# Retention and a snake feed-forward on one core: where transposes, stores, loads, one product, one relay and one output piece stand in the program of batches 1 to 4

## The chip, the core and the metric

The kernel runs on one core of a Trainium2 chip. The metric is the device time of one launch in microseconds (us). Before the change the median of three runs is 295.25 us (295.24, 295.25 and 296.3). A change of about 0.5% (1.5 us) is what a measurement of this kernel can tell from none.

The engines are named as in the profile: PE is the matrix engine (PEld its weight loads), DVE the vector engine, ACT the scalar engine, POOL the GpSimd engine, SP the engine that only issues DMAs. Each runs its own list of instructions in order; they meet at semaphores.

## The reference

```python
def _attn_ref(q, k, v):               # batch 8, heads 8, sequence 576, head size 64
    scores = scale * np.matmul(q, k.transpose(0, 1, 3, 2))
    rel = pos[:, None] - pos[None, :]
    Dmat = np.where(rel >= 0, gamma[:, None, None] ** rel[None, :, :], 0.0)
    return np.matmul(scores * Dmat, v)

def _moe_ref(x, w_in, w_out, alpha):  # x: 4608 tokens x 512; hidden size 2048
    h = x @ w_in
    s = np.sin(alpha * h)
    g = h + s * s / (alpha + 1e-09)
    return g @ w_out
```

The retention output of all heads, laid side by side, is the `x` of the feed-forward part. Inputs and output are float32.

## The kernel before, in words

The tokens are worked in nine **blocks** of 512: block n < 8 is the first 512 tokens of batch n, block 8 gathers the last 64 tokens of all batches. The feed-forward part of a block is cut into sixteen **units** of 128 hidden features, and for each unit there is:

- `project(n, fc, tag, part)`: PE multiplies `w_in` with the block's `xT` into the PSUM bank `tag` (L541), in one piece of 512 tokens or in two parts of 256;
- `sine(n, fc)`: ACT takes the sine out of that bank (L549);
- `square(n, fc, eng)`: ACT, DVE or POOL squares it in SBUF (L558, or L560 on DVE and POOL);
- `product(n, fc)`: DVE joins the square with the bank into `gT` (L565). Only then is the bank free for the next unit.

For blocks 0 and 1 the second matrix product is `gemm2(n, u, tag)` (L587): piece u of 16 does four of the sixteen hidden chunks of the 128-token column c = u // 4, and four pieces fill one bank. `finish(n, c)` copies that bank to an SBUF tile (L102 on ACT, L104 on DVE) and issues two stores on SP (L580). From block 2 on, seven products with sums and differences of weights take its place (`multiply`, L658); the weight differences come from `weigh` on POOL (L608).

Retention of batch b is done in two halves p of 256 tokens. `load(b, nm, p)` issues the 512 KB load of k, q or v on SP (L121); `cast(b, nm, p, eng, ys)` scales and narrows it to f16 on DVE or POOL (L181; plain for v: L102, L104), `ys` picking halves of the heads; from batch 2 on `crossed(b, p, nms)` issues a DMA transpose on SP (L205) that makes `kT` or `qT`. Then come `scores` (L363), `masked` (L375, DVE), `values` (L406), and the running state: `outer` (L298), `take_sum`, `next_sum`, `more` and `to_state` (L102, L327, L344, L345, L332), `add_states` (L428) and `keep`, which writes the block's `xT`.

`told(last, eng)` puts an empty instruction on an engine that waits for `last`, so that the engine goes no further until then (L250). With `relay=A_`, `values(p, False, ...)` puts such an instruction on ACT, and `values(p, True)`, which writes the same bank's other rows, waits for it on PE.

The order of everything is written out by hand between L746 and L1483 under a manual schedule: each call appends to the lists of the engines that it uses, in the order of the text. The change touches that list at L885 to L903 (units 10 to 15 of block 0), L969 to L1018 (end of batch 1, start of block 1, casts and transposes of batch 2, loads of batch 3) and L1118 to L1127 (transposes of batch 3, first load of batch 4). All SP work goes through one queue in that order.

Of the kernel before, what the change touches and what calls it, by code (L numbers as in the profile page):

```python
# [18 lines left out]
def kernel(  # L19
# [16 lines left out]
    nc = tc.nc  # L36
# [51 lines left out]
    V, A_, G_ = nc.vector, nc.scalar, nc.gpsimd  # L88
# [8 lines left out]
    def halves(n):  # L97
        return slice(64 * n, 64 * n + 64)
# [39 lines left out]
    def cast(b, nm, p, eng, ys=(0, 1)):  # L138
        t_ = raw[b, nm, p]
        if (b, nm, p) not in half:  # L140
            if p < 2:
                if nm == "k":
                    d_ = work.tile([P, 16 * D], F16, tag=f"k16{slot(b, p)}", bufs=1, name="k16")
                elif nm == "q":
                    n = order_of_q.index((b, p)) % 3 if b < 5 else 1 - p
                    d_ = work.tile([P, 16 * D], F16, tag=f"q16{n}", bufs=1, name="q16")
                else:
                    d_ = work.tile([P, 16 * D], F16, tag="v16", bufs=4, name="v16")
                d_ = (
                    d_.rearrange("p (h r d) -> p h r d", r=2, d=D)  # L150
                    if nm == "v"
                    else d_.rearrange("p (a r t d) -> p a r t d", a=4, r=2, t=2)
                )
            elif nm == "v":
                d_ = work.tile([P, H, D], F16, tag="vs16", bufs=B // 2, name="vs16")
            else:
                tag, n = ("qks16", 2) if b % 4 == 0 else (f"k16{int(nm == 'q')}", 1)
                d_ = work.tile([P, 4, 2, D], F16, tag=tag, bufs=n, name=nm + "s16")
            half[b, nm, p] = d_
        dst = half[b, nm, p]  # L160
        if p == 2:
            if nm == "v":
                copy(eng, dst.rearrange("p h d -> p (h d)"), t_.rearrange("p h d -> p (h d)"))
            else:
                eng.tensor_tensor(
                    dst.rearrange("p a t d -> p t a d"),
                    t_.rearrange("p (t a) d -> p t a d", t=2),
                    fac_s[nm].rearrange("p (t a) -> p t a", t=2).unsqueeze(3).to_broadcast([P, 2, 4, D]),
                    MULT,
                )  # L170
        elif nm == "v":
            h0, h1 = 4 * ys[0], 4 * ys[-1] + 4
            copy(
                eng,
                dst[:, h0:h1].rearrange("p h r d -> p (h r d)"),
                t_[:, h0:h1].rearrange("p h x -> p (h x)"),
            )
        else:
            a0, a1 = 2 * ys[0], 2 * ys[-1] + 2
            n = 2 * (a1 - a0)  # L180
            return eng.tensor_tensor(  # L181
                dst[:, a0:a1].rearrange("p a r t d -> p t (a r) d"),
                t_.rearrange("p (t a) x -> p t a x", t=2)[:, :, a0:a1].rearrange("p t a (r d) -> p t (a r) d", r=2),
                fac["halved k" if nm == "k" and b >= HALVED else nm]
                .rearrange("p (t x) -> p t x", t=2)[:, :, 2 * a0 : 2 * a1]
                .unsqueeze(3)
                .to_broadcast([P, 2, n, D]),
                MULT,
            )
# [58 lines left out]
    def told(last, eng):  # L248

        mark = eng.nop()  # L250
        order(mark, last)
        return mark
# [280 lines left out]
    def project(n, fc, tag, part=None):  # L533

        if n not in gT:
            gT[n] = work.tile([P, 2, FC, 256], F16, tag="gT", bufs=2, name="gT")
        if (n, fc) not in hps_of:
            hps_of[n, fc] = [bank(tag), None]
        cols = PART[part]
        for a in range(KT):  # L540
            matmul(  # L541
                hps_of[n, fc][0][:, cols], w_in16[:, a, fc * P : (fc + 1) * P], xs[n][:, a, cols],
                start=(a == 0 and part != 1), stop=(a == KT - 1), skip_group_check=True,
            )
# [9 lines left out]
    def square(n, fc, eng):  # L554
        s_t = hps_of[n, fc][1]
        ss_t = work.tile([P, 512], F16, tag="ss", bufs=4, name="ss_t")
        if eng is nc.scalar:
            nc.scalar.activation(ss_t, s_t, mybir.ActivationFunctionType.Square)  # L558
        else:
            eng.tensor_tensor(ss_t, s_t, s_t, MULT)  # L560
        hps_of[n, fc][1] = ss_t

    def product(n, fc):
        hps, ss_t = hps_of.pop((n, fc))
        nc.vector.scalar_tensor_tensor(  # L565
            gT[n][:, :, fc, :], ss_t.rearrange("p (t n) -> p t n", t=2), inva[:, fc : fc + 1],
            hps.rearrange("p (t n) -> p t n", t=2), MULT, ADD,
        )

    def rows_of(n, c):  # L570
        if n == 8:
            return out.rearrange("(b s) d -> b s d", s=S)[2 * c : 2 * c + 2, 512:576, :]
        r0 = 576 * n + 128 * c
        return out[r0 : r0 + 128, :].rearrange("(i r) d -> r i d", r=2)

    def finish(n, c, eng=None, cols=slice(0, 512), issue=(nc.sync, nc.sync)):
        osb = work.tile([P, 512], F32, tag="osb", bufs=4, name="osb")
        copy(eng or nc.scalar, osb[:, cols], ops[n, c, cols.start][:, cols])
        for r in range(2):
            issue[r].dma_start(rows_of(n, c)[r, :, cols], osb[halves(r), cols])  # L580

    def gemm2(n, u, tag, cols=slice(0, 512)):
        c, part = divmod(u, 4)
# [162 lines left out]
    with tc.manual_schedule():  # L746
# [139 lines left out]
        project(0, 10, "m0")  # L886
        sine(0, 10)
        square(0, 10, G_)
        told(cast(1, "k", 0, V, (1,)), G_)
        project(0, 11, "op")  # L890
        sine(0, 11)
        square(0, 11, A_)
        product(0, 10)
        product(0, 11)
        project(0, 12, "h2")
        sine(0, 12)
        square(0, 12, G_)
        project(0, 13, "h0")
        sine(0, 13)
        square(0, 13, A_)  # L900
# [69 lines left out]
        at[1].outer((1,), "m0")  # L970
        at[1].next_sum(2)
        at[1].to_state(2, V)
        at[1].take_sum(3, A_)
        at[1].values(1, False, "m1", relay=A_)
        gemm2(0, 7, "op")
        at[1].values(1, True)
        at[1].add_states(1)
        at[1].keep(1, A_)
        finish(0, 1)
        cast(2, "k", 1, V, (1,))  # L980
        cast(2, "k", 0, V)
        crossed(2, 0, "k")
        crossed(2, 1, "k")
        at[1].more(3)
        at[1].to_state(3, G_)
        cast(2, "v", 0, G_)
# [4 lines left out]
        weigh(2, 0, G_)  # L991
        project(1, 0, "m0", 0)
        project(1, 1, "h2", 0)
        project(1, 0, "m0", 1)
        sine(1, 0)
        project(1, 1, "h2", 1)
        square(1, 0, V)
        sine(1, 1)
        gemm2(0, 3, "h0")
        product(1, 0)  # L1000
        cast(2, "q", 0, V)
        crossed(2, 0, "q")
        load(3, "k", 1)
        finish(0, 0)
        square(1, 1, A_)
        project(1, 2, "m1", 0)
        project(1, 2, "m1", 1)
# [3 lines left out]
        project(1, 3, "h0")  # L1011
        sine(1, 3)
        crossed(2, 1, "q")
        load(3, "q", 1)
        load(3, "v", 0)
        load(3, "k", 0)
# [99 lines left out]
        sine(1, 15)  # L1116
        cast(3, "v", 1, A_, (0,))
        cast(3, "k", 0, V, (1,))  # L1118
        load(4, "k", 0)
        crossed(3, 0, "k")  # L1120
        cast(3, "v", 0, G_, (0,))
        cast(3, "v", 1, G_, (1,))
        at[2].more(3)
# [390 lines left out]
```

## Time and profile before

| | |
|---|---|
| median of the runs | 295.25 us (295.24 to 296.3) |
| the profiled execution | 296.25 us, of which the span of its instructions is 294.5 us |
| PE busy | 280.7 us, 95% of the span, granted clock 1.00 |
| DVE, ACT, POOL busy | 217.1, 211.3, 207.9 us |
| moved by DMA | 49.89 MB, mean 169 GB/s over the span |

In rows of the timeline the first two numbers are the start and the length in us, then engine, source line, operation, written tile <- read tiles, shape and how many instructions in a row were merged; what stands in square brackets is the idle time of the engine just before and what ended it. In the table of waits, the three numbers are the total in us, how many times, and the longest. Line numbers are those of the kernel before; in the changed kernel, lines from 582 on are six to eight higher.

### The profile page before, as it was taken

The numbers are of one execution on the slowest core, as the hardware profiler recorded it, in microseconds if no ns is written. First come the engines' busy times: TensorE is split into PE (matmuls) and PEld (weight loads), VectorE is DVE, ScalarE is ACT, GpSimd is POOL, SyncE is SP. The second block draws the span as 40 slices with busy tenths as digits, with TensorE's granted clock in tenths as the row PEclk, the third lists the DMA queues.
The fourth block names the chain that finished last, engine by engine and source line by source line (L and its number), as shares of the span: only waits on it lengthen the run. The fifth ranks groups of instructions, "written<-read, shape, count | busy, mean of one in ns | idle before, by whom it ended". The sixth has DMA issues, their size and how long they took to land.

```text
span 294.5 us, 8771 instructions
## 1 busy us (share of the span) xinstructions
PE 280.7 (95%) x3611; PEld 184.3 (63%) x3611; DVE 217.1 (74%) x299; ACT 211.3 (72%) x343; POOL 207.9 (71%) x198
## 2 busy tenths in 40 slices
PE   6799999989799999999999999999999999999993
PEld 5574455566544666676666666666666666665782
DVE  3859859999666689989686967686778495747861
ACT  3859733976849898787777778787868879887600
POOL 4888868999999989999997799679915800460000
PEclk9999999999999999999999999999999999999999
DMA  7999999999997887978798785778657101311225
GB/s 225 291 250 223 280 238 296 215 188 296 224 261 249 112 191 175 273 181 184 175 251 165 164 231 129 93 162 182 141 114 168 43 4 38 71 38 27 59 47 119
DMA packets 119159, 49.89 MB, mean 169 GB/s; under 512 B 69824, under 2 KB 118096, under 8 KB 119120
## 3 DMA queue, kind: packets, MB, share of 16 engines
q1 hardware_dynamic: 114528, 45.04, 65.2%
q0 software_dynamic: 4224, 4.19, 8.6%
q8 instruction: 28, 0.46, 0.7%
q10 hardware_dynamic: 368, 0.11, 0.2%
q14 instruction: 11, 0.09, 0.1%
HBM read 36.74 MB, written 9.44 MB: 157 GB/s over the span
## 4 chain that ended last, share of the span: by engine, by line
PE 75%; POOL 7%; DVE 6%; DMA 4%; ACT 3%; issue 2%; SPq 1%; ACTq 0%; POOLq 0%
PE hps L541 32%; PE hps L658 29%; PE ops L587 6%; DVE gT L565 2%; POOL T L608 2%; PE o L406 2%; PE sc L363 2%; DMA k<-in_k_dram 2%; DVE ret L375 2%; DMA qT<-q 2%; DVE k L181 2%; ACT s_t L549 1%; SPq L121 1%; POOL q L181 1%; PE kv L298 1%
## 5 line engine op out<-in xcount | busy, mean ns | idle before, releaser
L565 DVE SCALAR_TENSOR_TENSOR gT<-ss_t,inva,hps 128x512 f16<-128x512 f16 x144 | 105.2, 744 | 41.0 <-ACT ss_t L558 39.3
L549 ACT ACTIVATE s_t<-hps,alpha_t 128x512 f16<-128x512 f32 x144 | 96.5, 681 | 37.4 <-PE hps L541 37.0
L541 PE MATMUL hps<-xT,w_in 128*128 128x512 f16 (+1 forms) x604 | 121.3, 347 | 0.3
L541 PEld LDWEIGHTS <-w_in 128*128 128x128 f16 x668 | 63.7, 98 | 50.4 <-issue 1.2
L558 ACT ACTIVATE ss_t<-s_t 128x512 f16<-128x512 f16 x121 | 75.7, 630 | 3.4
L658 PEld LDWEIGHTS <-gT 128*128 128x128 f16 x656 | 63.9, 98 | 14.5
L630 POOL TENSOR_TENSOR gT<-gT,d 128x1024 f16<-128x1024 f16 x12 | 25.6, 2151 | 26.7 <-PE hps L658 26.0
L658 PE MATMUL hps<-T,gT 128*128 128x256 f16 x336 | 39.8, 273 | 0.0
L375 DVE TENSOR_TENSOR ret<-sc,mask 128x1024 f16<-128x1024 f32 (+1 forms) x32 | 35.0, 1119 | 6.4 <-PE sc L363 6.4
L658 PE MATMUL hps<-w_out,gT 128*128 128x256 f16 x320 | 38.2, 273 | 0.0
L678 DVE TENSOR_TENSOR osb<-osb,hps 128x512 f32<-128x512 f32 x35 | 24.0, 685 | 12.6 <-PE hps L658 11.3
L587 PE MATMUL ops<-w_out,gT 128*128 128x512 f16 x128 | 30.8, 380 | 0.7 <-DVE gT L565 0.7
L636 POOL TENSOR_TENSOR gT<-gT 128x1024 f16<-128x1024 f16 x12 | 25.3, 2128 | 0.0
L181 POOL TENSOR_TENSOR q<-q,cn 128x1024 f16<-128x1024 f32 (+1 forms) x16 | 25.2, 1590 | 0.1
L332 POOL TENSOR_TENSOR s<-kvs,cn 128x256 f16<-128x256 f32 x22 | 14.6, 664 | 8.2 <-ACT kvs L102 7.4
L587 PEld LDWEIGHTS <-gT 128*128 128x128 f16 x128 | 11.8, 98 | 13.1 <-issue 0.9
L345 POOL TENSOR_TENSOR kvs<-s,kvs 128x256 f32<-128x256 f32 x23 | 18.7, 812 | 1.8
L181 POOL TENSOR_TENSOR k<-k,cn 128x1024 f16<-128x1024 f32 (+1 forms) x11 | 18.8, 1709 | 0.0
L102 ACT COPY osb<-hps 128x512 f32<-128x512 f32 (+2 forms) x15 | 8.2, 549 | 13.5 <-PE hps L658 13.3
L102 ACT CAST xT<-o 128x1024 f16<-128x1024 f32 (+1 forms) x14 | 13.8, 989 | 4.0 <-PE o L428 4.0
L344 POOL TENSOR_TENSOR s<-kvs,cn 128x256 f32<-128x256 f32 x23 | 15.5, 673 | 1.6 <-DVE kvs L327 1.4
L541 PE MATMUL hps<-xS,w_in 128*128 128x512 f16 x64 | 15.0, 379 | 0.0
(78 smaller groups left out, 271.1 us busy)
## 6 DMA issues: line engine op xcount, KB each, us to landing
out_dram<-osb SPq DMA_DIRECT2D x70, 128.0 KB, 2.5
q<-in_q_dram SPq DMA_DIRECT2D x16, 512.0 KB, 6.0
k<-in_k_dram SPq DMA_DIRECT2D x10, 512.0 KB, 5.8
v<-in_v_dram SPq DMA_DIRECT2D x10, 512.0 KB, 6.6
k<-in_k_dram SPq DMA_DIRECT2D x24, 128.0 KB, 3.4
v<-in_v_dram SPq DMA_DIRECT2D x24, 128.0 KB, 3.6
w_in<-in_moe_w_in_dram POOLq DMA_DIRECT2D x4, 512.0 KB, 9.1
w_out<-in_moe_w_out_dram POOLq DMA_DIRECT2D x4, 512.0 KB, 9.5
```

The costliest lines, as they stand in the source:

```text
L102: eng.copy(d_, s_)
L181: return eng.tensor_tensor(dst[:, a0:a1].rearrange("p a r t d -> p t (a r) d"), t_.rearrange("p (t a) x -> p t a x", t=2)[:, :, a0:a1].rea ...
L375: made = nc.vector.tensor_tensor(ret.rearrange("p t (z x) -> p (t z) x", z=2)[:, :, 0:n], sc.rearrange("p t (z x) -> p (t z) x", z=2)[:, : ...
L541: matmul(hps_of[n, fc][0][:, cols], w_in16[:, a, fc * P : (fc + 1) * P], xs[n][:, a, cols], start=(a == 0 and part != 1), stop=(a == KT - ...
L549: nc.scalar.activation(s_t, hps, mybir.ActivationFunctionType.Sin, bias=0.0, scale=alpha_t[:, fc : fc + 1],)
L558: nc.scalar.activation(ss_t, s_t, mybir.ActivationFunctionType.Square)
L565: nc.vector.scalar_tensor_tensor(gT[n][:, :, fc, :], ss_t.rearrange("p (t n) -> p t n", t=2), inva[:, fc : fc + 1], hps.rearrange("p (t n) ...
L587: matmul(ops[n, c, cols.start][:, cols], gT[n][:, c // 2, fk, c % 2 * P : c % 2 * P + P], w_out16[:, fk, cols], start=(fk == 0), stop=(fk ...
L630: eng.tensor_tensor(self.part(0, 0, i), self.part(1, 1, i), self.d3[:, 4 * i : 4 * i + 4], SUB)
L636: eng.tensor_tensor(out_, self.part(1, 0, i), self.part(0, 0, i), SUB)
L658: matmul(self.ps[name][:, 256 * m + cols.start : 256 * m + cols.stop], left(j)[:, P * m : P * m + P], right(j)[:, cols], start=(tag is not ...
L678: nc.vector.tensor_tensor(out_, a, self.ps[ps], ADD)
```

## The change

Some pieces of work stand at other places of the list. What is computed and the number of instructions stay the same.

1. Block 0: `product(0, 11)` goes between the two DVE halves of the cast of k of batch 1, ahead of `product(0, 10)`. POOL's wait for the second half (`told`) goes behind POOL's square of unit 12.
2. Batch 1: the relay on ACT goes ahead of the copy of the fourth sum (`take_sum(3, A_)`).
3. Batch 2: the transpose of k, half 0, goes ahead of the stores of `finish(0, 1)`, and the transpose of k, half 1, behind the transpose of q, half 0, and the stores of `finish(0, 0)`.
4. Block 0's last piece of column 0, `gemm2(0, 3)`, goes ahead of the second parts of block 1's units 0 and 1; the copy of `finish(0, 0)` follows it on ACT, and only its stores (`store_0`) stay at the old place.
5. The load of k of batch 3, half 1, goes behind the last transpose of batch 2.
6. The transpose of k of batch 3, half 0, goes ahead of the first load of batch 4.

```diff
+    def finish(n, c, eng=None, cols=slice(0, 512), issue=(nc.sync, nc.sync), hold=False):
         osb = work.tile([P, 512], F32, tag="osb", bufs=4, name="osb")
         copy(eng or nc.scalar, osb[:, cols], ops[n, c, cols.start][:, cols])
-        for r in range(2):
-            issue[r].dma_start(rows_of(n, c)[r, :, cols], osb[halves(r), cols])
+        def store():
+            for r in range(2):
+                issue[r].dma_start(rows_of(n, c)[r, :, cols], osb[halves(r), cols])
+        if hold:
+            return store
+        store()
...
         square(0, 10, G_)
-        told(cast(1, "k", 0, V, (1,)), G_)
         project(0, 11, "op")
         sine(0, 11)
         square(0, 11, A_)
+        product(0, 11)
+        cast_k = cast(1, "k", 0, V, (1,))
         product(0, 10)
-        product(0, 11)
         project(0, 12, "h2")
         sine(0, 12)
         square(0, 12, G_)
+        told(cast_k, G_)
...
+        at[1].values(1, False, "m1", relay=A_)
         at[1].take_sum(3, A_)
-        at[1].values(1, False, "m1", relay=A_)
...
-        finish(0, 1)
         cast(2, "k", 1, V, (1,))
         cast(2, "k", 0, V)
         crossed(2, 0, "k")
-        crossed(2, 1, "k")
+        finish(0, 1)
...
         project(1, 0, "m0", 0)
         project(1, 1, "h2", 0)
+        gemm2(0, 3, "h0")
+        store_0 = finish(0, 0, hold=True)
         project(1, 0, "m0", 1)
         sine(1, 0)
         project(1, 1, "h2", 1)
         square(1, 0, V)
         sine(1, 1)
-        gemm2(0, 3, "h0")
         product(1, 0)
         cast(2, "q", 0, V)
         crossed(2, 0, "q")
-        load(3, "k", 1)
-        finish(0, 0)
+        store_0()
+        crossed(2, 1, "k")
...
         crossed(2, 1, "q")
+        load(3, "k", 1)
         load(3, "q", 1)
...
         cast(3, "k", 0, V, (1,))
+        crossed(3, 0, "k")
         load(4, "k", 0)
-        crossed(3, 0, "k")
```

On DVE, at the casts of k of batch 1 (tile `k_635`, from the loaded `k_361`), between the products of block 0 (`gT`):

```order
 L565 SCALAR_TENSOR_TENSOR gT<-ss_t,inva,hps 128x2x256 x9
-L181 TENSOR_TENSOR k_635<-k_361,cn 128x2x4x64 x2
-L565 SCALAR_TENSOR_TENSOR gT<-ss_t,inva,hps 128x2x256 x4
+L181 TENSOR_TENSOR k_635<-k_361,cn 128x2x4x64
+L565 SCALAR_TENSOR_TENSOR gT<-ss_t,inva,hps 128x2x256
+L181 TENSOR_TENSOR k_635<-k_361,cn 128x2x4x64
+L565 SCALAR_TENSOR_TENSOR gT<-ss_t,inva,hps 128x2x256 x3
```

One product (unit 11) now stands between the two halves of the cast, and the second half is one product later.

On ACT, at the end of batch 1 and the start of block 1: `xT` is what `keep(1)` writes, the `osb` copies are those of `finish(0, 1)` and `finish(0, 0)`, the first two `s_t` the sines of block 1's units 0 and 1, `ss_t` the square of unit 1:

```order
 L102 CAST xT<-o 128x4x256
-L102 COPY osb<-ops 128x512
-L549 ACTIVATE s_t<-hps,alpha_t 128x512 x2
-L102 COPY osb<-ops 128x512
+L102 COPY osb<-ops 128x512 x2
+L549 ACTIVATE s_t<-hps,alpha_t 128x512 x2
 L558 ACTIVATE ss_t<-s_t 128x512
```

The copy of `finish(0, 0)` moved from behind the two sines to ahead of them.

On SP, from the stores of `finish(0, 3)` to the first loads of batch 3, before (`k_1100` and `q_1155` are half 0 of batch 2, `k_999` and `q_1114` half 1; `k_1159` is the load of k of batch 3, half 1):

```order
L580 DMA out_dram<-osb 64x512 x4
L205 DMA_TRANSPOSE kT<-k_1100 128x8x128
L205 DMA_TRANSPOSE kT<-k_999 128x8x128
L205 DMA_TRANSPOSE qT<-q_1155 128x8x128
L121 DMA k_1159<-in_k_dram 128x8x128
L580 DMA out_dram<-osb 64x512 x2
L205 DMA_TRANSPOSE qT<-q_1114 128x8x128
```

and now (`k_1096` is half 0 of k, `q_1112` half 1 of q, `k_1188` the load):

```order
L582 DMA out_dram<-osb 64x512 x2
L205 DMA_TRANSPOSE kT<-k_1096 128x8x128
L582 DMA out_dram<-osb 64x512 x2
L205 DMA_TRANSPOSE qT<-q_1155 128x8x128
L582 DMA out_dram<-osb 64x512 x2
L205 DMA_TRANSPOSE kT<-k_999 128x8x128
L205 DMA_TRANSPOSE qT<-q_1112 128x8x128
L121 DMA k_1188<-in_k_dram 128x8x128
```

The transposes of half 0 have a pair of stores between them and stand ahead of half 1's; the load moved from fifth entry to last, behind all four transposes and six stores.

More of the change, by code (lines that the diff above doesn't have):

```diff
@@ L574, in rows_of @@
         return out[r0 : r0 + 128, :].rearrange("(i r) d -> r i d", r=2)
-    def finish(n, c, eng=None, cols=slice(0, 512), issue=(nc.sync, nc.sync)):
+    def finish(n, c, eng=None, cols=slice(0, 512), issue=(nc.sync, nc.sync), hold=False):
         osb = work.tile([P, 512], F32, tag="osb", bufs=4, name="osb")
         copy(eng or nc.scalar, osb[:, cols], ops[n, c, cols.start][:, cols])
-        for r in range(2):
-            issue[r].dma_start(rows_of(n, c)[r, :, cols], osb[halves(r), cols])
+        def store():
[4 more added lines that the diff above has]
+        store()
     def gemm2(n, u, tag, cols=slice(0, 512)):
```

## The prediction

> **What bounds the kernel now.** I read the page first: the shares of the engines and of the chain that ended last.
>
> ```profile
> PE 280.7 (95%) x3611; PEld 184.3 (63%) x3611; DVE 217.1 (74%) x299; ACT 211.3 (72%) x343; POOL 207.9 (71%) x198
> PE 75%; POOL 7%; DVE 6%; DMA 4%; ACT 3%; issue 2%; SPq 1%; ACTq 0%; POOLq 0%
> ```
>
> PE is busy 95% of the span and carries 75% of the chain, so a change gains only where PE stands still. Next came what PE itself waited for, then the timeline of PE, which gives the place of each wait in the stretch that the change touches.
>
> ```profile
> PE sc L363 <- DMA qT<-q: 2.5, 2, 1.5
> PE ops L587 <- DVE gT L565: 0.7, 1, 0.7
> PE o L406 <- ACTq L250: 0.2, 1, 0.2
> ```
>
> ```profile
> 32.35 1.02 PE L587 MATMUL ops<-w_out,gT 128*128 128x512 f16 x4 [0.66 <-DVE gT L565]
> ...
> 50.09 0.42 PE L406 MATMUL o<-ret,v 64*64 64x128 f16 x16 [0.15 <-ACTq L250]
> ...
> 62.45 0.42 PE L363 MATMUL sc<-qT,kT 64*64 64x128 f16 x16 [1.01 <-DMA qT<-q]
> ...
> 80.16 0.42 PE L363 MATMUL sc<-qT,kT 64*64 64x128 f16 x16 [1.50 <-DMA qT<-q]
> ```
>
> Four waits, 3.32 us together, and the edits point at all four: the product behind two cast halves (0.66), the relay (0.15), and two scores that wait for a transposed q (1.01 and 1.50). With 0.31 of one late weight load (below) that is the most that can be gained, 3.6 us. From 80.16 to the end the rows of PE show no wait over 0.15 us, so what PE has gained there it should keep.
>
> **Edit 1, the product between the cast halves.**
>
> ```profile
> 29.38 1.00 DVE L181 TENSOR_TENSOR k<-k,cn 128x512 f16<-128x512 f32 x1
> ...
> 30.30 0.68 DVE L181 TENSOR_TENSOR k<-k,cn 128x512 f16<-128x512 f32 x1
> 30.90 2.71 DVE L565 SCALAR_TENSOR_TENSOR gT<-ss_t,inva,hps 128x512 f16<-128x512 f16 x4
> ...
> 28.79 1.04 POOL L560 TENSOR_TENSOR ss_t<-s_t 128x512 f16<-128x512 f16 x1 [0.77 <-ACT s_t L549]
> 31.11 1.04 POOL L560 TENSOR_TENSOR ss_t<-s_t 128x512 f16<-128x512 f16 x1 [1.28 <-ACT s_t L549]
> ...
> 29.86 1.25 ACT L549 ACTIVATE s_t<-hps,alpha_t 128x512 f16<-128x512 f32 x2
> ...
> 33.65 1.89 PE L587 MATMUL ops<-w_out,gT 128*128 128x512 f16 x8
> ```
>
> The two halves of the cast are equal work, but the first took 1.00 us, the second 0.68. The first began while POOL's square (28.79 to 29.83) ran: about 0.3 us are the wait for it. Units 10 to 13 take 2.71 / 4 = 0.68 us each. PE, free at 31.69, waits for unit 11's product, which ends near 32.3 as the second of the four.
>
> Now unit 11 ends near 31.0 and the first wait goes. But the second half is ready at 30.95, and POOL's square of unit 12 no longer stands behind it: it starts when its sine is done (the first of the two at 29.86, so near 30.6) and runs to 31.6. If it holds up the half-cast as the earlier square did, that ends at 31.5 + 0.68 = 32.2, unit 10 at 32.9, unit 12 at 33.5, unit 13 at 34.2. PE's transpose of k needs unit 10's bank: 32.9. The next piece, at 33.65 before, needs unit 12's bank: 33.55. So 0.66 is won and 0.56 given back: **0.1 us**. With no such hold-up the half-cast ends at 31.65 and the whole 0.6 us stays; the bounds are 0 and 0.66. I take 0.1, by the row nearest to it, the 1.00 us half.
>
> On this the Trainium skill, page "SBUF — State Buffer", section "SBUF: two separate sides", has a rule that speaks against the edit: VectorE instructions with two SBUF inputs and GpSimd instructions share a pair of ports, "an exclusive lock, not a bandwidth split", and the loser waits to the end. The trace agrees with it here (1.00 beside the square, 0.68 alone). By the rule the edit gives 0.1 us, without it 0.6.
>
> **Edit 2, the relay.** 0.15 us of wait goes; `add_states` behind it waits for a DVE state that isn't moved, so I count 0 to 0.15, taken as 0.1, the smaller part being hidden.
>
> **Edit 4, the output piece ahead of unit 0's end.**
>
> ```profile
> 51.85 0.75 PEld L541 LDWEIGHTS <-w_in 128*128 128x128 f16 x7 [0.31 <-issue]
> ...
> 51.69 0.59 ACT L102 COPY osb<-ops 128x512 f32<-128x512 f32 x1
> 52.48 1.27 ACT L549 ACTIVATE s_t<-hps,alpha_t 128x512 f16<-128x512 f32 x2 [0.20 <-PE hps L541]
> 53.78 0.59 ACT L102 COPY osb<-ops 128x512 f32<-128x512 f32 x1
> ...
> 53.47 1.23 POOL L104 CAST v<-v 128x1024 f16<-128x1024 f32 x1
> ...
> 54.65 2.04 POOL L104 CAST v<-v 128x1024 f16<-128x1024 f32 x1
> ...
> 56.66 2.07 POOL L181 TENSOR_TENSOR q<-q,cn 128x1024 f16<-128x1024 f32 x1
> ...
> 145.09 1.04 POOL L104 CAST v<-v 128x1024 f16<-128x1024 f32 x1
> ...
> 53.20 0.60 DVE L560 TENSOR_TENSOR ss_t<-s_t 128x512 f16<-128x512 f16 x1
> ...
> 54.57 1.22 DVE L181 TENSOR_TENSOR q<-q,cn 128x1024 f16<-128x1024 f32 x1
> ...
> 56.37 0.60 DVE L560 TENSOR_TENSOR ss_t<-s_t 128x512 f16<-128x512 f16 x1
> 57.07 0.75 DVE L565 SCALAR_TENSOR_TENSOR gT<-ss_t,inva,hps 128x512 f16<-128x512 f16 x1
> ...
> 98.11 0.43 DVE L560 TENSOR_TENSOR ss_t<-s_t 128x512 f16<-128x512 f16 x1 [1.13 <-ACT s_t L549]
> ...
> 71.45 1.90 POOL L181 TENSOR_TENSOR q<-q,cn 128x1024 f16<-128x1024 f32 x1
> ```
>
> On PE the piece fills the wait for `xT` (0.31). Its copy, though, now stands ahead of the two sines on ACT. The piece starts near 51.5 and is done near 52.5, four matmuls of 0.22 and the drain; the copy starts at 52.5, the first sine at 53.0 instead of 52.48. DVE's square of unit 0 is ready at 53.75 instead of 53.20.
>
> That half microsecond changes who comes first. The casts of v take 1.04 us on POOL alone, but 1.23 and 2.04 here: the first waited for DVE's square, the second (from 54.65) for DVE's cast of q (to 55.79). In the same way 0.17 of the 2.07 of POOL's cast of q, 1.90 alone, went behind DVE's second square. They take turns. With the square at 53.75 POOL's first v cast (53.47 to 54.5) is ahead of it. Step by step, an instruction getting in some 0.13 us before the other's end is shown: square 54.4 to 54.8 (0.43 alone), POOL's second v cast 54.7 to 55.7, product of unit 0 to 55.5, DVE's cast of q 55.6 to 56.8, POOL's cast of q 56.7 to 58.6, product of unit 1 to 57.5. The square of unit 2 is ready at 57.4, in the middle of POOL's 1.90 us: 58.5 to 58.9. Product of unit 2 ends at 59.65 instead of 57.82, **1.83 us later**. If none of them held the other up it would be 0.5 us later; the bounds are 0 and 1.83, and all three POOL rows say the upper one.
>
> ```profile
> 57.87 0.79 PEld L541 LDWEIGHTS <-w_in 128*128 128x128 f16 x8 [0.30 <-DVE gT L565]
> ```
>
> Here PE already waits for that product: unit 6 reuses its bank (m1). So PE, at that place near 57.5, stands until 59.7: 1.8 us late. The work from there to the scores took 3.5 us (57.9 to 62.45 less the wait of 1.01): PE arrives at 63.2 instead of 62.45, **0.7 us behind**, with the second wait gone but paid for in the bank.
>
> **Edits 3 and 5, the order on SP.**
>
> ```profile
> 54.75 2.75 SPq L205 DMA_TRANSPOSE kT<-k  x2
> 57.60 1.25 SPq L205 DMA_TRANSPOSE qT<-q  x1
> 58.90 1.99 SPq L121 DMA_DIRECT2D k<-in_k_dram  x1
> ...
> 62.25 1.39 SPq L205 DMA_TRANSPOSE qT<-q  x1
> ...
> 73.39 1.30 SPq L205 DMA_TRANSPOSE kT<-k  x1
> 74.80 1.72 SPq L205 DMA_TRANSPOSE qT<-q  x1
> ...
> 67.49 1.04 POOL L181 TENSOR_TENSOR k<-k,cn 128x512 f16<-128x512 f32 x1
> ```
>
> A transpose takes SP 1.25 us, a pair of stores between the load and the next transpose at most 1.36 (60.89 to 62.25). The q of half 0 goes out at 56.9 (the DVE cast ends at 56.8) instead of 57.60, and was in 4.8 us after issue (57.60 to 62.4, when the scores start): 61.7, ahead of PE's 63.2. Then a pair of stores (58.2 to 59.4), k and q of half 1 (to 62.0), and the load of k of batch 3 at 62.05, 3.15 us later than at 58.90. The other five loads follow at once, where before they began only at 63.69, after 62.25 + 1.39; so the last load, the stores and the transposes of batch 3 half 1 come about 1 to 1.5 us sooner. The transpose of q there can go when POOL's cast is done (71.45 + 1.90 = 73.35), at 73.4 instead of 74.80, and 5.3 us of flight (74.80 to 80.12 before) bring it in at 78.7. PE was there at 80.16 - 1.50 = 78.66 and now arrives at 79.35. The last wait of 1.50 goes, and 0.8 of it remains as gain.
>
> **Edit 6** puts a transpose ahead of a load; its scores come seven microseconds later and show no wait: nothing.
>
> **The sum.** 80.16 becomes 79.35: 0.8 us (the 3.6 us of waits become 2.8: 0.56 left at edit 1, 0.05 at the relay, and 2.2 new ones at the bank). The profiled execution, 296.25 us with its 294.5 us of span and 1.75 around it, becomes 295.45. The runs' median is 1.00 below it; the same 0.8 gives **294.4 us**.
>
> **Rivals.**
>
> *The engines don't get into each other's way at the new places.* Then unit 2's product is only 0.5 us late or not at all, edit 1 gives its 0.6 and PE arrives at the last scores near 77.9, with q in by then: 2.3 us, **292.9 us**. Against it stand the 1.00, 2.04 and 2.07 us rows; for it, that the order turns on 0.28 us (53.47 against 53.75) and that the worked-out times are no better than 0.1 or 0.2.
>
> *The load of k comes too late, on the slower side.* POOL reads it at 67.49, and POOL then works without a pause to the cast of q. From 62.05 that leaves 5.4 us. Loads of k in this stretch took 5.8 and 7.2 us:
>
> ```profile
> DMA to landing us min/median/max: 5.8/6.5/7.2
> ...
> v<-in_v_dram SPq DMA_DIRECT2D x2, 512.0 KB, 8.3
> ```
>
> The second row is of the v loads at 45 to 55 us. At 5.8 POOL waits 0.4 us, still hidden, since q would be in at 79.1. At 7.2 it waits 1.8, q comes at 80.5 and the kernel is 0.3 us slower. It decides from 6.9 us of flight on; at 8.5 us, near that second row, it is **296.8 us**, 1.6 slower. For it: six DMAs stand ahead that didn't before. Against it: they are short, and the queue ahead holds no 512 KB load any more.
>
> *DVE's cast of q loses its turn to POOL's* (0.27 us between them): unit 2's product another 1.1 us later, and 0.2 to 0.3 us slower than now, 295.5 us.
>
> **How the numbers follow.** The forecast, 0.50, has its own range of 293.8 to 295.1. The first rival has 0.30 (292.6 to 293.7), the late load 0.14 (295.5 to 297.5, most of it above 296.7 only with a long flight), the lost turn 0.06. A measurement here tells about 0.5%, 1.5 us. Faster by more: 0.30. Slower by more: 0.10 of the late load's and 0.02 of things not thought of, 0.12. Same: 0.58. The range 292.6 to 296.3 leaves out 0.05 below and 0.14 above. That the runs' median is 1.00 under the profiled execution speaks for the upper half of it: if that microsecond is in the waits that go, less is to be had.
>
> **What would show it.** In the changed profile: PE's row after the first transposes at 33.5 or 33.0 (edit 1); the length of the second half-cast, 1.2 or 0.68; a PE wait of about 2 us for DVE gT L565 (some lines lower) near 57.5, and a DVE square of about 1.5 us ahead of it; no PE wait for DMA qT at either place; POOL's cast of k of batch 3 without a wait for a DMA. I am wrong if the wait near 57.5 is missing (then it is faster), or if PE still waits at the last scores with POOL idle before 67.5 (then it isn't).

## The result, and the profile after

The changed kernel is slower: a median of 297.38 us (296.17 to 298.56, 15 runs) against 294.98 us (294.02 to 296.83, 15 runs) of the kernel before beside it, a ratio of 1.008 with a 95% interval of 1.0058 to 1.0103. Forecast were 294.4 us, and at most 296.3.

The profiled execution of the changed kernel took 296.85 us, with a span of 295.1. From its page, the busy shares, the granted clock in 40 slices and the chain:

```profile
PE 282.7 (96%) x3611; PEld 185.4 (63%) x3611; DVE 219.9 (75%) x299; ACT 211.2 (72%) x343; POOL 207.6 (70%) x198
PEclk9999999979999999999999999999999999999999
PE 77%; DVE 9%; DMA 5%; ACT 3%; issue 2%; SPq 2%; POOL 1%; ACTq 0%; DVEq 0%
```

PE is busy 2 us longer than before (282.7 against 280.7) with the same 3611 matmuls, which by itself says little, since two further profiles of the kernel before have 281.4 and 282.6. One slice of the clock, the ninth, shows 7. Two lines of PE's waits, and PE's timeline at the places of the four old ones:

```profile
PE hps L541 <- DVE gT L565: 1.9, 1, 1.9
...
PE tr L215 <- DVE gT L565: 0.4, 1, 0.4
```

```profile
32.94 0.61 PE L215 MATMUL tr<-ident,k 128*128 128x128 f16 x8 [0.35 <-DVE gT L565]
33.60 0.59 PE L593 MATMUL ops<-w_out,gT 128*128 128x512 f16 x2
...
59.66 1.63 PE L541 MATMUL hps<-xT,w_in 128*128 128x256 f16 x8 [1.95 <-DVE gT L565]
61.23 1.07 PE L298 MATMUL kv<-v,k 64*64 64x64 f16 x64
62.23 2.47 PE L541 MATMUL hps<-xT,w_in 128*128 128x256 f16 x16
64.62 0.42 PE L363 MATMUL sc<-qT,kT 64*64 64x128 f16 x16
...
80.70 0.41 PE L363 MATMUL sc<-qT,kT 64*64 64x128 f16 x16
```

Up to 59.66 these are the forecast's rows to a tenth. Then the times of PE's work stretch: eight matmuls that take 1.05 us elsewhere take 1.63, and the scores, awaited at 63.2, begin at 64.62. The windows of this kernel say why (start:end, length, PE busy and count, granted clock, DMA share, GB/s):

```profile
55.00:60.00 5.00, 3.05 (x16) 1.00 0.73 160
60.00:65.00 5.00, 5.00 (x104) 0.66 1.03 148
```

Behind the wait of 1.95 us PE ran at half its clock for 3.41 us (59.97 to 63.38 in the trace's clock record). Both waits for `qT` are gone, as forecast, but PE starts the last scores of batch 2 at 80.70, where it started them at 80.16 before.

That explains 0.54 us, and the medians are 2.4 apart. So the experiments had two questions: what the clock, the wait and the order on SP each cost, and why the kernel before is mostly faster than its profiled execution.

### The profile page after: what moved, and what is told of

Read it like the earlier page. It is cut to its first block, busy times and chain, and to the rows that moved or that the text cites. A ratio compares the mean times of both kernels' runs of the same rounds, so it can differ in the third digit from the quotient of the medians.

```text
span 295.1 us, 8771 instructions
## 1 busy us (share of the span) xinstructions
PE 282.7 (96%) x3611; PEld 185.4 (63%) x3611; DVE 219.9 (75%) x299; ACT 211.2 (72%) x343; POOL 207.6 (70%) x198
## 4 chain that ended last, share of the span: by engine, by line
PE 77%; DVE 9%; DMA 5%; ACT 3%; issue 2%; SPq 2%; POOL 1%; ACTq 0%; DVEq 0%
PE hps L541 33%; PE hps L664 29%; PE ops L593 7%; DVE gT L565 4%; PE o L406 2%; PE sc L363 2%; DMA v<-in_v_dram 2%; DMA k<-in_k_dram 2%; ACT s_t L549 2%; SPq L121 2%; DVE k L181 2%; PE kv L298 1%; DVE ss_t L560 1%; DVE ret L375 1%; DMA out_dram<-osb 1%
## 5 line engine op out<-in xcount | busy, mean ns | idle before, releaser
L181 POOL TENSOR_TENSOR q<-q,cn 128x1024 f16<-128x1024 f32 (+1 forms) x16 | 26.5, 1671 | 0.8 <-DVE k L181 0.7
L181 DVE TENSOR_TENSOR k<-k,cn 128x512 f16<-128x512 f32 (+1 forms) x12 | 13.3, 1129 | 3.9 <-DMA k<-in_k_dram 3.7
```

The source lines that it names most:

```text
L181: return eng.tensor_tensor(dst[:, a0:a1].rearrange("p a r t d -> p t (a r) d"), t_.rearrange("p (t a) x -> p t a x", t=2)[:, :, a0:a1].rea ...
```

## The experiments

All ratios are to runs of the kernel before taken along with them, with 95% intervals. "The last scores" are those that PE starts at 80.16 in the forecast's profile; they need the transposed q of batch 2, half 1, called `qT(3,1)` below by the numbers of the expectations.

**The kernel before, twice more.** No edit.

> The kernel before once more, for a second profile and for the spans and clocks of its single runs. If its runs differ by the two waits for the transposes of q (1.01 and 1.50 us in the first profile), a run of 294.1 shows them shorter by a microsecond or more in sum; if they differ by the granted clock, runs above 295.5 show a clock below 0.998.

> The kernel before for a third profile. If it falls on one of its runs near 294, it shows PE at the last scores of batch 2 near 77.7 to 78.2 with no wait for qT ahead of it, and qT(3,1) landing before that; if it falls on a run near 295 or above, a wait for qT or a late start of PE's first projection.

Measured: 295.24 us (293.91 to 296.97, 12 runs), ratio 1.0002 (0.998 to 1.0025), profiled span 293.4; and one run of 294.71 us, span 293.0. PE's timeline at the two scores that waited 1.01 and 1.50 us in the forecast's profile, first in the second profile of this kernel, then in the third:

```profile
62.58 0.42 PE L363 MATMUL sc<-qT,kT 64*64 64x128 f16 x16
...
79.10 0.41 PE L363 MATMUL sc<-qT,kT 64*64 64x128 f16 x16
```

```profile
61.51 0.42 PE L363 MATMUL sc<-qT,kT 64*64 64x128 f16 x16
...
78.60 0.42 PE L363 MATMUL sc<-qT,kT 64*64 64x128 f16 x16 [0.38 <-DMA qT<-q]
```

In the second profile neither wait is there; in the third the first is missing and the second is 0.38. So the 2.51 us that the forecast set out to win belong to one execution. From the start of the last scores to the end all three take the same: 294.5 - 80.16 = 214.4, 293.4 - 79.10 = 214.3, 293.0 - 78.60 = 214.4. The time of this kernel is **the start of the last scores plus 214.4**, and that start is the later of PE's own arrival and the landing of `qT(3,1)`. In the third profile the landing comes last (78.56). In the second it is PE: the landing is at 78.80, and PE is late because its clock record has 3.41 us at a granted clock of 0.5, from 13.76 to 17.17; at the first of the two scores it is 1.07 us behind the third profile. The expected reason for the short runs, neither wait, stays open, since no profile of this kernel fell on a run near 294. The other expected reason, the clock, is on record: of 112 runs of the kernel before in the experiments, 30 have a mean granted clock below 0.995 and a median of 295.56 us, 55 have 0.998 or more and a median of 294.49.

**Edit 4 taken out, and edit 4 alone.** The first as a diff to the changed kernel; the second has these lines the other way round, in the kernel before.

```diff
-        gemm2(0, 3, "h0")
-        store_0 = finish(0, 0, hold=True)
         project(1, 0, "m0", 1)
...
         sine(1, 1)
+        gemm2(0, 3, "h0")
+        store_0 = finish(0, 0, hold=True)
```

> The kernel after with edit 4 undone alone: gemm2(0,3) stands again behind the sine of unit 1 of block 1, and the copy of finish(0,0) behind both sines; edits 1, 2, 3, 5 and 6 stay. First theory (the wait that edit 4 makes, and the clock): the wait of 1.95 us at 57.71 is gone, no stretch at a granted clock of 0.5 behind it, PE reaches the last scores of batch 2 near 79.0 to 79.4 instead of 80.70, and the time is 2 to 3 us below the kernel after, 0 to 0.9 us below the kernel before. Second theory (the order of SP's transposes, stores and loads costs the time): the time stays within 0.5 us of the kernel after, 297.4. Third (the two k waits that the SP order removes are short in most runs of the kernel before, so that nothing was to be won there): the time is that of the kernel before within 0.4 us.

> The kernel before with edit 4 alone: gemm2(0,3) ahead of the second parts of units 0 and 1 of block 1, the copy of finish(0,0) ahead of the two sines, its stores where they were. First theory: the same turns of DVE and POOL, the product of unit 2 ends near 59.6, PE waits 1.5 to 2 us for it and the granted clock falls to 0.5 for some microseconds in many of the runs; the time is 2 to 3 us above the kernel before. Second theory (SP's order is to blame): within 0.5 us of the kernel before.

Measured: without edit 4, 295.69 us, ratio 1.0037 (1.0015 to 1.0059); edit 4 alone, 296.44 us, ratio 1.0046 (1.0027 to 1.0066). So edit 4 by itself costs 1.3 us. On top of the rest of the change it costs 1.7 by the first 15 runs of the changed kernel and 1.0 by the six later ones (296.72, below), neither of which was taken along with the kernel without it. What is left of the change does not gain but loses another 0.5 by the medians, 1.1 by the ratio. The expectation's first theory had a gain there; it falls for that half. Edit 4 alone shows the same wait and the same clock in its profile, which is the longest of its seven runs (297.58 us); first the timeline, then the windows:

```profile
59.70 1.62 PE L541 MATMUL hps<-xT,w_in 128*128 128x256 f16 x8 [1.95 <-DVE gT L565]
```

```profile
60.00:65.00 5.00, 5.00 (x103) 0.66 1.13 204
```

**The copy back behind the sines, the piece left ahead.**

```diff
         gemm2(0, 3, "h0")
-        store_0 = finish(0, 0, hold=True)
...
         sine(1, 1)
+        store_0 = finish(0, 0, hold=True)
```

> The kernel after with only the copy of finish(0,0) put back behind the sines of units 0 and 1; the piece gemm2(0,3) stays ahead. It tells the early copy on ACT from the early piece on PE. If the copy makes the wait (as the prediction had it): DVE's square of unit 0 starts near 53.2, the product of unit 2 ends near 57.9, no PE wait of 1.95 us at 57.71, no granted clock of 0.5, and a median within 0.5 us of the kernel without edit 4, 295.7. If the piece makes it: wait and clock as in the kernel after, 297.4.

Measured: 296.51 us, ratio 1.0061 (1.0041 to 1.0081). DVE's timeline, then PE's:

```profile
53.71 1.02 DVE L560 TENSOR_TENSOR ss_t<-s_t 128x512 f16<-128x512 f16 x1 [0.71 <-ACT s_t L549]
...
57.29 1.47 DVE L560 TENSOR_TENSOR ss_t<-s_t 128x512 f16<-128x512 f16 x1
58.86 0.75 DVE L565 SCALAR_TENSOR_TENSOR gT<-ss_t,inva,hps 128x512 f16<-128x512 f16 x1
```

```profile
51.49 1.03 PE L593 MATMUL ops<-w_out,gT 128*128 128x512 f16 x4
52.35 1.91 PE L541 MATMUL hps<-xT,w_in 128*128 128x256 f16 x16
54.78 1.89 PE L541 MATMUL hps<-xT,w_in 128*128 128x512 f16 x8 [0.52 <-ACT osb L102]
...
59.67 1.05 PE L541 MATMUL hps<-xT,w_in 128*128 128x256 f16 x8 [1.27 <-DVE gT L565]
```

The squares are as late as in the changed kernel (53.76 and 57.29 there). It is the **piece on PE** that makes them late: with it at 51.49 the second parts of units 0 and 1 come at 52.35, and unit 0's sine starts at 52.99 without the copy ahead of it. The place of the copy only moves part of the wait to another bank: 0.52 and 1.27, and no stretch at half clock.

**PE kept busy through the wait.** Nine spare matmuls into an unused bank, read by nobody, and the changed kernel beside it.

```diff
+        idle = psum.tile([P, 512], F32, tag="h2", bufs=1, name="idle")
+        for _ in range(9):
+            matmul(idle, w_in16[:, 0, 0:P], xs[1][:, 0, :], start=True, stop=True)
         project(1, 6, "m1", 0)
```

> The kernel after with nine matmuls of 128x512 into a spare bank ahead of the first part of unit 6 of block 1 (some 1.9 us of work that nobody reads), where PE waited 1.95 us for the product of unit 2. The wait of DVE and POOL for each other is as before; only PE isn't idle in it. First theory with the clock as its half: no granted clock of 0.5 behind it, PE at scores(0,1) near 63.2 instead of 64.62, and the median 1 to 2 us below the kernel after, still some 0.5 to 1.5 us above the kernel before. If the wait alone carries the loss and the clock nothing: within 0.4 us of the kernel after.

> The kernel after once more: a median 2.0 to 2.8 us above the kernel before; the wait of 1.95 us at 57.7 again, and behind it a granted clock of 0.5 for 3.4 us in some of the runs, with a mean clock near 0.994 in those; a run without it has 0.999 or more and is 1 to 1.7 us shorter.

> The kernel after with the nine spare matmuls in the wait, once more, beside after_again. If the halved clock has the share that the first pair of runs gave it: a median 0.8 to 1.5 us below after_again. If that was chance: within 0.4 us of it.

Measured: filled 296.22 us, ratio 1.0051 (1.0032 to 1.007), and on another chip 296.50, ratio 1.0055 (1.0034 to 1.0076). The changed kernel beside the second was 296.72 us, ratio 1.0059 (1.0041 to 1.0076): 1.8 us above the kernel before, where 2.0 to 2.8 were expected. Against the first pair's difference of 1.16 us, whose two kernels were not run side by side, stands 0.22 of the second, inside both intervals. PE's timeline of the changed kernel's second profile has the explanation; its clock is 1.00 throughout:

```profile
59.50 1.05 PE L541 MATMUL hps<-xT,w_in 128*128 128x256 f16 x8 [1.95 <-DVE gT L565]
...
62.97 0.42 PE L363 MATMUL sc<-qT,kT 64*64 64x128 f16 x16
...
80.14 0.42 PE L363 MATMUL sc<-qT,kT 64*64 64x128 f16 x16 [0.96 <-DMA qT<-q]
```

With the full clock PE is at 62.97, 1.65 us sooner than in the first profile, and then waits 0.96 for `qT(3,1)`, which lands at 80.09. Filled does the same (landing 80.01). Between the two profiles the halved clock is worth 0.56 us, 80.70 - 80.14: with it PE comes last, without it the landing does.

Over the runs a lower clock goes with more than that. Nine of the first 15 runs of the changed kernel have a mean granted clock of 0.994 or less and a median of 297.70 us, six have 0.998 or more and 296.41. Of the six later runs two have 0.994 or less, and the median of the other four is 296.62. So the two series agree at the full clock, some 2 us above the 294.49 of the kernel before, and that is what the landing has to explain. Why the clock was lower in more of the first runs is open; the filled kernel, too, has runs at 0.991 to 0.995.

**The orders on SP, apart.** Edits 3, 5 and 6 without the rest; edit 5 alone; edit 3 alone; and the change without edits 4 and 5. The core of them: the load is edit 5, the transpose of k, which comes from behind `crossed(2, 0, "k")`, edit 3.

```diff
         crossed(2, 0, "q")
-        load(3, "k", 1)
         finish(0, 0)
+        crossed(2, 1, "k")
...
         crossed(2, 1, "q")
+        load(3, "k", 1)
```

> The kernel before with edits 3, 5 and 6 alone (the order of SP's transposes, stores and loads). First theory now (each landing of qT(2,0) and qT(3,1) is set by whether a 16 KB fetch of PE's own instructions falls into its packets, not by its place among loads and stores): the time stays within 0.5 us of the kernel before, and the wait for qT(3,1) can still be there (the kernel without edit 4 showed 1.44 us of it). Theory of the prediction (both waits go with the order): 0.8 us or more below the kernel before. Third (the late load of k pushes the loads of batch 3 and so the transposes behind them): 0.4 to 0.9 us above the kernel before, as the kernel without edit 4 was, with no part of that from edits 1 and 2.

> The kernel before with edit 5 alone: the load of 512 KB of batch 3's second k issued behind the last transpose of batch 2 instead of ahead of it. Theory now (that load moves from a stretch where the DMA engines have room, 58 to 64 us, into one where they are full, 64 to 75 us, so that all of batch 3's loads and qT(3,1) behind them come about a microsecond later): qT(3,1) lands at 79.0 or later, PE waits 1 us or more for it, and the median is 0.5 to 1.0 us above the kernel before. Rival (the place of the load means nothing, edits 3 or 6 did it): within 0.3 us of the kernel before.

> The kernel before with edit 3 alone. Theory now (with the second k transpose behind four stores and the q transpose, all that SP issues from 58 us on comes some 0.4 us later, and qT(3,1), bound by SP's queue and the DMA engines, lands 0.5 to 0.9 us later, at 79.0 to 79.4): PE waits 1.0 to 1.4 us for it, and the median is 0.4 to 0.9 us above the kernel before. Rival (edit 6 costs it: the transpose of kT(3,0) competes with the packets of qT(3,1)): within 0.3 us of the kernel before, the wait near 0.4 to 0.6.

> The kernel after without edits 4 and 5: edits 1, 2, 3 and 6 stay, the load of k goes ahead of the transposes again. Theory now: the loads of batch 3 are through a microsecond earlier than without edit 4 alone, so the median falls by 0.5 to 1.0 us from that kernel's 295.7, to that of the kernel before or up to 0.4 below it, since edits 1 and 2 save 0.2 us on PE. Rival (edit 3 delays the transposes by itself): it stays 0.3 us or more above the kernel before.

Measured: edits 3, 5 and 6, 295.49 us, ratio 1.0030 (1.0012 to 1.0048); edit 5, 294.92 us, ratio 1.0009 (0.999 to 1.0028); edit 3, 295.48 us, ratio 1.0016 (1.0002 to 1.003); 1, 2, 3 and 6, 295.23 us, ratio 1.0026 (1.0007 to 1.0044). Edit 5 by itself is nothing that can be measured, against the theory of its expectation. Edit 3 costs: alone (by little, 1.0002), and in the three other kernels that have it without edit 4, the interval lies above 1. How much of the difference to 1.0030 is edit 5's or 6's the intervals leave open. SP's timeline (issues) of the kernel before, third profile:

```profile
61.34 1.32 SPq L205 DMA_TRANSPOSE qT<-q  x1
62.70 0.58 SPq L121 DMA_DIRECT2D q<-in_q_dram  x1
...
68.05 1.39 SPq L121 DMA_DIRECT2D q<-in_q_dram  x1
69.54 2.03 SPq L580 DMA_DIRECT2D out_dram<-osb  x2
71.68 1.41 SPq L205 DMA_TRANSPOSE kT<-k  x1
73.51 1.32 SPq L205 DMA_TRANSPOSE qT<-q  x1
```

the same queue with edits 3, 5 and 6:

```profile
58.42 2.16 SPq L205 DMA_TRANSPOSE kT<-k  x1
60.69 1.25 SPq L205 DMA_TRANSPOSE qT<-q  x1
61.99 0.58 SPq L121 DMA_DIRECT2D k<-in_k_dram  x1
...
68.87 1.39 SPq L121 DMA_DIRECT2D q<-in_q_dram  x1
70.36 2.03 SPq L582 DMA_DIRECT2D out_dram<-osb  x2
72.49 1.37 SPq L205 DMA_TRANSPOSE kT<-k  x1
73.97 1.88 SPq L205 DMA_TRANSPOSE qT<-q  x1
```

and in the changed kernel, second profile:

```profile
56.61 1.24 SPq L205 DMA_TRANSPOSE qT<-q  x1
...
59.17 1.36 SPq L205 DMA_TRANSPOSE kT<-k  x1
60.63 2.22 SPq L205 DMA_TRANSPOSE qT<-q  x1
62.91 0.59 SPq L121 DMA_DIRECT2D k<-in_k_dram  x1
...
69.85 1.46 SPq L121 DMA_DIRECT2D q<-in_q_dram  x1
...
73.54 1.41 SPq L205 DMA_TRANSPOSE kT<-k  x1
75.06 1.67 SPq L205 DMA_TRANSPOSE qT<-q  x1
```

In 15 of the 18 profiles the first two loads of this row take SP 0.56 to 0.83 us each to issue, and every load behind them 1.31 to 3.08. In the third profile the DMA engines move 163 GB/s from 58 to 61 us and 318 to 341 from 65 to 71; that the full engines hold the queue back is read from this, not tested. Edit 5 puts a sixth load into the row, so four issues are long instead of three, and the last load goes out at 68.87 instead of 68.05. In the changed kernel the row and what follows it are another 0.9 to 1.1 us later, and the delay begins at the first q transpose: 56.61 instead of 55.81. That one needs DVE's cast of q, here with the orders alone and then in the changed kernel:

```profile
54.53 1.22 DVE L181 TENSOR_TENSOR q<-q,cn 128x1024 f16<-128x1024 f32 x1
```

```profile
55.33 1.22 DVE L181 TENSOR_TENSOR q<-q,cn 128x1024 f16<-128x1024 f32 x1
```

Edit 4 makes the cast 0.8 us late, and since edit 3 the second k transpose, and all that follows on SP, stands behind it. So the two halves of the change meet on SP. A single profile's issue times vary, so here are those of 15 profiles (issue and landing of `qT(3,1)`, start of the last scores):

| kernels | issue | landing | last scores |
|---|---|---|---|
| before, three profiles | 73.51 to 74.80 | 78.56 to 80.12 | 78.60 to 80.16 |
| edits 1 and 2; edit 5 | 73.61, 73.63 | 78.50, 78.52 | 78.54, 78.56 |
| edit 3 in it, not 4 (four kernels) | 73.97 to 74.70 | 79.01 to 79.48 | 79.05 to 79.53 |
| edits 3, 4 and 5 (changed kernel twice, filled twice, copy put back) | 74.88 to 75.24 | 78.37 (once), 80.01 to 80.13 | 80.05 to 80.70 |
| edit 4 alone | 73.33 | 76.82 | 80.72 |

Edit 4 alone has the transpose early and is held by PE, in an execution with the halved clock; what holds its other runs no profile shows. With the orders PE waits for the landing in four of the five profiles, and the fifth is the one with the halved clock. The third row lies within the first, so that edit 3 costs by a later issue is argued from the order of the queue and not shown by these times: the runs show that it costs, and the profile of edit 3 alone has a halved clock of its own, from 13.88 to 17.29 us.

**Edits 1 and 2 alone.** The diff is that of the change.

> The kernel before with edits 1 and 2 alone, the two short waits of PE. The prediction had them at 0.1 us each. Theory now: PE is 0.1 to 0.2 us earlier from 50 us on, and where a wait for qT follows it takes that back; the median within 0.3 us of the kernel before, on either side. Rival (edit 1's lock of DVE and POOL, or the relay on ACT, costs more than the waits): 0.3 us or more above.

Measured: 294.49 us, ratio 1.0006 (0.9988 to 1.0024). PE's wait of 0.66 us is 0.35 in its profile, its arrival at the last scores earlier, and the landing of `qT(3,1)` (a wait of 0.51) takes it back.

**PE's instructions moved against the program.** The 46 warm-up matmuls on zeros made 22, in the kernel without edit 4 and in the kernel before.

```diff
-        keep_busy(16, "h0", 256)
-        keep_busy(14, "op", 64)
+        keep_busy(8, "h0", 512)
+        keep_busy(7, "op", 128)
...
-        keep_busy(4, "h1", 256)
+        keep_busy(2, "h1", 512)
```

> The kernel without edit 4, whose 46 warm-up matmuls on zeros at the start are made 22, wider, so that they take about as long. Nothing else moves but PE's instruction count: a fetch of 16 KB (256 instructions, so 128 matmuls with their weight loads) comes 24 matmuls later in the program. In the kernel without edit 4 the fetch near matmul 1041 came at 75.73, among the packets of qT(3,1), which landed at 79.36. If the fetch sets that landing: it comes near 77.3 here, qT(3,1) lands near 78.0 to 78.4, the wait of 1.44 us for it is 0 to 0.5, and the median falls by 0.4 to 1.2 us against the kernel without edit 4. If the fetch is only a bystander: the wait and the median stay within 0.3 us.

> The kernel before with the same 24 matmuls fewer at the start. If the fetches set the two waits for qT: the fetch that came at 58.87 among the packets of qT(2,0) comes later (PE is at its matmul 755 of before then, near 59.1 to 59.6, so it can still hit), the one at 76.51 comes near 78, and the median falls by 0.3 to 1 us towards the 294.1 of the best runs. If not: within 0.3 us of the kernel before.

Both came out the other way: 297.85 us, ratio 1.0117 (1.0084 to 1.0151), and 296.92 us, ratio 1.0072 (1.0047 to 1.0096). The fetch near the last scores did not move in the program (76.39 and 76.12), so these runs say nothing on what it does to `qT(3,1)`. They show another thing, in PE's timeline of the second:

```profile
98.61 0.35 PE L406 MATMUL o<-ret,v 64*64 64x128 f16 x12
100.54 0.25 PE L406 MATMUL o<-ret,v 64*64 64x128 f16 x4 [1.58 <-issue]
```

PE stops in the middle of a row of sixteen equal matmuls, for nothing that the profile names; a fetch of its instructions had begun at 97.6, where the kernel before had it near 93. Stops of this kind of 0.2 us or more occur six times in the 18 profiles, and counted over PE's matmuls and weight loads all six stand 193 or 194 instructions behind a multiple of 256: at 2753 and 3522 in both of these kernels, at 2241 in edit 4 alone and at 2242 in the second filled one. A fetch of 16 KB is made for every 256 or so (last section), so they fit a wait for the next one; that is read from the traces, not tested. In these two kernels the rest behind the last scores is 215.8 (without edit 4) and 216.0 us instead of 214.4.

**A version with the transposes ahead.** Edits 1 and 2, the stores of `finish(0, 2)` behind the two transposes, and one weight difference of POOL behind the casts of batch 3.

```diff
-        weigh(2, 0, G_)
...
-        finish(0, 2, V)
+        store_2 = finish(0, 2, V, hold=True)
...
         crossed(3, 1, "k")
         crossed(3, 1, "q")
+        store_2()
...
+        weigh(2, 0, G_)
         weigh(2, 1, G_)
```

> The kernel before with edits 1 and 2, the stores of finish(0,2) issued behind the two transposes of batch 3 instead of ahead of them, and one of POOL's weight differences (2.3 us) moved from ahead of batch 3's k and q casts to behind them. If the landing of qT(3,1) near 78.5 bounds the kernel before: the transpose is issued 1.5 to 2.5 us earlier, lands at 76 to 77.5 and PE's wait of 0.4 to 0.6 us for it goes; the median falls by 0.3 to 0.7 us, to 293.9 to 294.3. If it doesn't bound: within 0.2 us of the kernel before.

Measured: 294.48 us against 294.96, ratio 0.9988 (0.9969 to 1.0007). SP's timeline, then PE's:

```profile
69.23 3.30 SPq L205 DMA_TRANSPOSE kT<-k  x1
72.64 1.32 SPq L205 DMA_TRANSPOSE qT<-q  x1
```

```profile
77.57 0.48 PE L363 MATMUL sc<-qT,kT 64*64 64x128 f16 x16
```

The transpose went out 0.9 us earlier than in the third profile of before, less than the 1.5 to 2.5 expected; it landed at 77.44, PE did not wait, and the last scores started at 77.57 instead of 78.60. The median's gain of 0.5 us is of the expected size, but the interval holds 1: that it beats the kernel before is not shown.

## Why the prediction was wrong, point by point

- **Edit 1** was right: PE's wait 0.35 instead of 0.66, the next piece at 33.60 (forecast 33.55). **Edit 2** too; its wait is gone. Together they are worth nothing in the time (1.0006).
- **Edit 4**: the size was right, the cause half wrong. "Product of unit 2 ends at 59.65" came true (PE starts behind it at 59.66), and so did the DVE and POOL turns behind it. But "its copy, though, now stands ahead of the two sines" is not the reason; the piece ahead of the second parts is, as the kernel with the copy put back shows.
- **"PE arrives at 63.2 instead of 62.45"**: 62.97 at full clock, 64.62 in the execution where the clock halved. The term for the clock was missing. Its net price between the two profiles is 0.56 us; over the first 15 runs those with a low mean clock are 1.3 us longer.
- **Edits 3 and 5, the step that failed**: "the last load, the stores and the transposes of batch 3 half 1 come about 1 to 1.5 us sooner". They come no sooner: the q transpose was issued at 74.88 and 75.06, where the profile before had 74.80 and the forecast 73.4, and it landed at 80.09 in the second profile, where the forecast had 78.7. Two terms of the sum were too small. The transposes of k and q of half 1 were put at 2.6 us (59.4 to 62.0) and took 3.38 and 3.68, so the row of loads began at 62.76 and 62.91 instead of 62.05. And the six loads, now all in one row, took SP 8.51 and 8.40 us, where the forecast leaves 7.6 to 8.1 (from 62.05 to 1 to 1.5 us ahead of 71.15, the end of the old row). The delay of DVE's cast of q it had right: 56.9 for the transpose behind it, 56.78 and 56.61 in the two profiles. The forecast also compared this row with one execution; in the third profile of before the transpose was out at 73.51.
- **"The last wait of 1.50 goes, and 0.8 of it remains"**: in other executions of the kernel before that wait is 0.38 or nothing. The base was one execution, 1.27 us above the median of the 15 runs; the last sentence on the range names this danger, and the sum did not follow it.
- The rival on the slower side had the right sign and place (SP's loads of batch 3) but another mechanism: POOL waited only 0.27 us for its k in the first profile and not at all in the second, and the q transpose was late in SP's queue.

In all: edit 4 alone 1.0046, the rest without it 1.0037, together about the 1.008 measured. The six later runs give 1.0059, less than that sum. Not settled is edit 6's share, what holds edit 4 alone at the full clock, and why more of the first 15 runs had a low clock, which is where their median's 0.66 us above the six later ones comes from as far as the record shows.

## What to carry to other kernels

A wait seen in one profile may belong to that execution: take a second profile, or compare the span with the fastest runs, before you count on winning it. When a wait for a transfer ends a stretch, the price of every edit ahead of it goes through the queue that issues the transfer, so work that queue out issue by issue, with the longer issue times that a row of loads has behind its second. Moving a piece of work into an idle place of PE delays what stood behind it by as much of the piece as the idle time does not cover, whatever happens to its copy; here that was 0.5 us at unit 0's sine (52.99 instead of 52.48).

## What the runs showed of the hardware

- **A short wait can halve the clock.** 1.95 us of idle PE, twice with 3.41 us at a granted clock of 0.5 behind it (changed kernel, first profile; edit 4 alone), and once with none (second profile, same wait). In the kernel before, second profile, a stretch of the same 3.41 us begins at 13.76, behind waits of at most 0.97 us from 10 us on; the third profile has 0.91 there and the full clock. What decides is not shown. The Trainium skill, page "TensorE: Matmul & The Clock Gate", section "HAM oscillation — how this bites in real kernels", gives as the rule to avoid idle gaps above some 3.4 us. Here a gap of 1.95 us was enough, and the measurement decides.
- **PE's instruction fetches share the DMA engines.** The page of the changed kernel's profile has them as a queue, with its share of the 16 engines:

```profile
q8 instruction: 28, 0.46, 0.6%
```

28 packets of 16 KB, for 3611 matmuls and as many weight loads: one per 256 or so, which is the block that the Trainium skill, page "Runtime: NRT & Kernel Launch", section "Instruction fetch mechanics", states. It calls their cost mostly hidden; if the stop of 1.58 us above is one, as its place suggests, that one is not. There is also a pattern in the flight of `qT(3,1)`. In the table of its tile it is, from issue to landing, for edit 4 alone

```profile
DMA to landing us min/median/max: 3.5/3.5/3.5
```

and for the changed kernel's second profile

```profile
DMA to landing us min/median/max: 5.0/5.0/5.0
```

It is 3.5 us in two profiles, in which the next fetch began at 78.6, behind the landing (76.82, edit 4 alone), and at 77.8, 0.6 us ahead of the landing (78.37, the changed kernel's first). It is 4.2 to 5.3 in the sixteen in which one began between 75.1 and 77.2, earlier in the flight. The two short ones are also the two with the halved clock at 60 us, so the fetch is not told apart from PE's lateness. The fetch comes as PE gets to about its 1040th matmul, so a PE that is earlier can meet the transpose with its own fetch. This is read from the traces; the runs that were to test it did not move the fetch.
